# Sixty-two narrow products of zeros ahead of the first scores, three weight loads moved forward, and a new issue order in an attention and feed-forward kernel

## The chip, the core and the metric

The kernel runs on one core of a Trainium2 chip. The metric is the device time of one execution in microseconds; lower is better. TensorE (PE) multiplies, VectorE (DVE) and ScalarE (ACT) work elementwise and empty the accumulators, GpSimd (POOL) only builds an identity matrix, and SyncE (SP) issues every data transfer.

## What is computed

Chunked attention: every chunk of 32 queries looks at 8 memory keys and at the keys from 16 before the chunk to 8 behind it. Its output goes through a two-layer feed-forward block of width 2048 with a piecewise quadratic activation.

```
for c in range(nc):                                   # 24 chunks of 32 queries
    k_full = concat(mem_k, k[c*32-16 : c*32+32+8])    # v_full likewise
    a = softmax(q_c @ k_full.T / sqrt(64))
    out[c] = a @ v_full
x = out.transpose(0, 2, 1, 3).reshape(3072, 512)
h = x @ w_in                                          # 512 x 2048
g = where(h >= 1, h, where(h <= -1, 0, (h + 1)**2 / 4))
return g @ w_out                                      # 2048 x 512
```

## The kernel before, in words

The 3072 tokens are cut into six blocks of 512. Products are made as sums of three products of split operands (high and low parts), so each feed-forward slice of 128 hidden columns (called fc, 0 to 15) takes 12 products for the first layer and 12 for the second. Blocks 0 and 1 go this direct way. Blocks 2 to 5 use seven products in place of eight on combined operands (a fast 2 by 2 scheme), some of which are saved to and read back from device memory.

The order of all work is written out by hand in two tables of short names, and every engine keeps the order in which the program issues its instructions (class `InOrder`, line 132). `FIRST` (line 29) covers blocks 0 and 1 and the start of block 2, `PLAN` (line 63) the rest. Each name steps one small generator forward, and a step issues the instructions of one operation, mostly on one engine.

The names of `FIRST` that matter here:
- `+` issues the next transfer of the list `early` (line 1080): keys and queries of the first block in four groups, values, and the sixteen weight pieces of 1 MB (`load_w`), then the keys (`load_qk`, 1.5 MB) and values (`load_v`, 1 MB) of block 1.
- `g0` to `g3` are the four head groups of block 0 (`first_attention`): 64 score products; a reduction to the maximum; its subtraction; the exponential on ScalarE; sum, addition, reciprocal and multiplication on VectorE; 4 transposes on TensorE; a copy on ScalarE; 64 value products; and the high and low part of the result (`xth` on ScalarE, `xtl` on VectorE). g0 and g1 make the first half of the tokens of block 0, g2 and g3 the second.
- `w0` to `w15` decode a weight piece (`decode`): a scaling on ScalarE, three steps on VectorE, the high part on ScalarE, the low part on VectorE.
- `A0`, `A1`, ... and `B0`, ... are half steps of the feed-forward block for the first and the second half of block 0 (12 products of 256 columns, three activations, and later 6 products into the output); `E4`, ... are whole steps.

Ahead of both tables `keep_warm(8)` issues eight products of a tile of zeros (`warm`, bf16, 128x512) into one of the two `ps_h` accumulators, while the first keys are on their way.

In `PLAN`, `42p6` is product 6 of the third slice of block 4; `42c3` copies an accumulator into a tile `gt`, of which there are two (`copy_out`); `42a22` adds to it; `42r22` applies the activations; `42m22` joins them and sends the result to device memory (`keep`). The tile `gt` is taken by `c1`, `c3` and `r21`, and is free again after the matching `m`. Names with a `u` are the second layer of blocks 3 to 5 (`4u1q3` is one of its products), those with an `x` or a `y` the attention of a block.

Of the kernel before, what the change touches and what calls it, by code (L numbers as in the profile page):

```python
# [27 lines left out]

FIRST = """
    + + g0 g0 g0 + g0 g1 g0 + g0 g0 g1 g1 g0 g1 + g1 g0 w0 g1 g1 + g1 g0 w0 g1 w0 + g0 g1 w0 w0 g2  # L30
    + g0 w0 g1 w1 g2 g1 g2 g3 + g0 g2 g1 A0 g2 g3 g2 g3 + g3 A1 A0 g2 + g2 + g3 g2 g3 + A1 w1 w2 g3
    w1 g2 w3 A0 g3 + g3 w2 g3 w1 w2 g2 + g3 g2 g2 A0 g3 g3 A1 B0 + w2 w4 w1 w1 A0 B0 w3 + A2 B0 A1
    w2 B1 A1 A2 + w3 B0 w2 B1 B2 B1 w4 w3 B1 w5 A2 + B1 B0 w3 A0 A3 B0 w7 A2 A1 w4 w3 A2 B2 w5 B2
    w6 w4 + B2 w5 B2 B3 B1 A3 E4 w4 A3 + w8 w4 + B3 w5 E5 B2 w9 + A3 + E4 w6 B3 w5 A2 w6 E4 w6 B3
    A3 A3 w5 B3 w10 w6 w7 w11 E4 B3 w6 E5 w7 w8 + w7 E5 E7 w13 w7 E5 w12 E6 + w8 w14 E4 E6 w15 w7
    E4 w8 w9 E6 E5 E8 E5 w9 w8 w9 E6 E7 E6 w9 E7 w9 E8 E5 w8 E6 E9 E7 E7 w10 w11 w10 E7 E8 E4 E9
    w10 E8 w10 E6 E8 w11 w10 + w11 w12 w11 E9 E7 w12 E10 w11 E9 n0 E8 E9 E8 E10 w12 E10 E11 w13 w12
    E10 w12 w13 n0 E10 w13 E11 + E12 E11 w13 n0 E9 w14 n0 E10 E11 w13 E12 n0 n0 E9 E10 E11 E11 E11
    n0 n0 E12 n0 n0 n0 n0 + E13 n0 E12 n0 w14 E13 w15 E12 w14 n0 w15 n0 n0 E14 E12 n1 w14 n0 C0 w14
    w15 n1 E13 E15 n1 E14 E12 w15 E13 E14 E13 n1 n1 n1 E14 w15 n1 C0 E15 E14 n1 + n1 E15 n1 E13 n1  # L40
    n1 n1 C1 n1 C1 C0 E13 E15 C2 E14 E15 E14 C1 n1 E15 n1 C2 E15 C0 n1 n1 E15 E15 C0 D0 E15 C2 E15
    C1 D1 C3 D0 C0 C1 t0 C2 D1 D3 t0 D0 C1 D0 t0 C3 t0 D2 t0 t0 t0 D0 F5 D1 C2 t0 t1 D3 t1 t1 C3 t1
    C3 t1 C3 D1 D0 t1 D2 F4 D3 D1 D2 D3 C3 D1 t1 t2 F6 t1 t2 C2 D3 t2 D3 t2 D2 D2 F4 F4 F5 t2 t2 t3
    F5 t2 t2 t3 t3 F4 F5 t3 F6 D2 F4 t3 t3 F5 t4 F7 t4 n2 t3 F5 F4 t3 F4 F7 t4 F6 F6 F7 F6 t4 t4 t4
    t4 F5 t5 t5 t4 t5 t5 F7 t5 n2 t5 F7 F6 t6 t5 t6 t5 F8 F8 n2 n2 F8 n2 F7 t6 F9 t6 F9 n2 t6 t6 n2
    t6 F8 t7 n2 F8 F10 F9 F9 F6 t6 t7 F11 n2 n2 n2 F7 t7 n2 n2 + F9 t7 n2 t7 F10 F8 F11 t7 F8 t7
    F10 F12 F11 n2 F10 F10 F9 + n2 n3 t7 F12 n3 n3 F11 n3 n3 F13 n3 F10 F11 n3 F10 F12 F12 n3 F9
    F11 F12 n3 n3 F13 F13 F11 + n3 F12 n3 F13 n3 n3 n2 F14 F14 F14 n3 F13 F15 F12 n3 F14 F13 F14 n3
    n2 F13 F15 F15 F15 F15 n3
# [19 lines left out]
    22p6 T3 22a11 T3 3y 3y 22c2 22p7 22r11 3y 3y 22m11 22c3 3y 21m11 21g12 22h11 22p5 22a22 22p4
    22l11 22r21 22p3 3y 20g12 3y 23p1 T0 3y 3y T3 T3 T3 22m21 22a12 3y 22h21 23p2 22l21 3y T0 23c1  # L70
    23p6 21h11 21l11 23a11 22r12 22m12 T0 21g22 3y 3y 22r22 T0 T0 T0 T3 3kA11 T0 T0 22m22 3y 21g11
    T3 23p5 T0 T3 T3 3y 22h12 22l12 T4 T4 T4 T4 23c2 23p7 22h22 3kA12 22l22 23r11 3jA12 T3 22g11 T3
    T4 23c3 3y 23a22 3dS3 3kS3 23r22 23m11 23h11 T4 T2 23p4 3dS1 3dS2 23l11 T2 23r21 23p3 T2 T2 T2
    T2 22g21 23m22 T2 T2 3jA11 3kS2 23g11 23a12 T2 T2 3dS4 22g12 3kA22 3jS2 3jA22 23h22 3kS4 30p1
# [1136 lines left out]
```

## Time and profile before

| | us |
|---|---|
| median of three runs (585.54 to 586.42) | 586.1 |
| the profiled execution | 588.56 |
| its span, first to last instruction | 586.8 |
| TensorE busy | 568.6 (97%) |
| VectorE busy | 495.5 (84%) |
| ScalarE busy | 361.9 (62%) |

The share of busy time is a mean over very different stages. TensorE's idle time and its slower clock lie almost wholly in the first fortieths of the span; from 44 us on it is hardly ever idle. During the first four fortieths the DMA engines are busy without a break with the weights.

### The profile page before, as it was taken

Reading aid. Unit: us, or ns where it says so; the run is one execution under the profiler, and the core shown is the slowest. Engines: PE = TensorE matmul, PEld = TensorE weight load, DVE = VectorE, ACT = ScalarE, POOL = GpSimd, SP = SyncE. Lnnn points to the kernel's source line nnn. Section 1 sums busy time; section 2 is a strip of 40 time slices with the busy share of each in tenths; the row PEclk is TensorE's granted clock in tenths of the full one; section 3 lists DMA queues with packets and bytes.
Section 4 is the critical chain, followed back from the end, with each engine's and each line's share of the span. In section 5 each row is a group of like instructions: output and inputs, shape, how many; then the busy total and the mean of one; then the engine's idle time right before and its main releaser. Section 6 shows DMA issues by size and latency. Waiting matters only on the chain.

```text
span 586.8 us, 15427 instructions
## 1 busy us (share of the span) xinstructions
PE 568.6 (97%) x6504; PEld 516.6 (88%) x6504; DVE 495.5 (84%) x854; ACT 361.9 (62%) x667; POOL 0.7 (0%) x6
## 2 busy tenths in 40 slices
PE   5889999999999999999999999999999999999997
PEld 2788788889888889989888899999999999999997
DVE  5789999996989778687999689999887988666895
ACT  2489955446546446656685677576677565667652
POOL 0000000000000000000000000000000000000000
PEclk8579999999999999999999999999999999999999
DMA  8999103254976763474165798887898868887241
GB/s 351 421 422 418 77 0 109 71 165 145 341 279 237 271 240 120 164 275 163 55 251 170 259 311 307 299 300 268 286 287 283 290 205 301 286 255 249 90 151 48
DMA packets 39492, 135.21 MB, mean 230 GB/s; under 512 B 4096, under 2 KB 4096, under 8 KB 34816
## 3 DMA queue, kind: packets, MB, share of 16 engines
q1 hardware_dynamic: 39424, 134.23, 64.7%
q8 instruction: 51, 0.84, 0.6%
q14 instruction: 17, 0.14, 0.1%
HBM read 106.95 MB, written 27.26 MB: 229 GB/s over the span
## 4 chain that ended last, share of the span: by engine, by line
PE 83%; DVE 10%; DMA 3%; ACT 2%; issue 1%; DVEq 0%; SPq 0%; ACTq 0%
PE ps_o L140 38%; PE ps_h L140 37%; PE ps_x L140 4%; PE ps_s L140 3%; DVE gs L140 1%; DVE pr L140 1%; DMA gr<-plain_g 1%; PE ps_g L140 1%; DVE pt L140 1%; DMA wr<-saved 1%; DVE den L140 1%; DMA qk<-in_first_qk_dram 1%; DVE mx L140 1%; DVE ob L140 1%; DVE gk L140 1%
## 5 line engine op out<-in xcount | busy, mean ns | idle before, releaser
L140 PE MATMUL ps_o<-wr,gh 128*128 128x512 f32 x384 | 120.8, 396 | 0.0
L140 PE MATMUL ps_h<-s,wr 128*128 128x256 f32 x720 | 94.3, 283 | 0.7 <-ACT gt L140 0.4
L140 PE MATMUL ps_h<-xth,wr 128*128 128x512 f32 (+1 forms) x320 | 92.4, 364 | 0.0
L140 PEld LDWEIGHTS ps_h<-s,wr 128*128 128x128 f32 x720 | 89.4, 188 | 1.9 <-ACT gt L140 0.6
L140 PEld LDWEIGHTS ps_o<-wr,gh 128*128 128x128 f32 x384 | 70.5, 188 | 15.3 <-ACT ob L140 0.2
L140 PE MATMUL ps_o<-wr,gl 128*128 128x512 f32 x192 | 75.7, 394 | 0.0
L140 PE MATMUL ps_h<-a,wr 128*128 128x256 f32 x540 | 71.3, 283 | 0.5 <-DMA wr<-saved 0.5
L140 PEld LDWEIGHTS ps_h<-a,wr 128*128 128x128 f32 x540 | 67.6, 188 | 1.6 <-DMA wr<-saved 0.7
L140 PEld LDWEIGHTS ps_h<-xth,wr 128*128 128x128 f32 x320 | 59.5, 200 | 9.8 <-ACT gt L140 0.5
L140 PE MATMUL ps_h<-xtl,wr 128*128 128x512 f32 (+1 forms) x160 | 56.2, 362 | 0.1
L140 DVE SCALAR_TENSOR_TENSOR gw<-gw,gt 128x512 f32<-128x512 f32 (+1 forms) x76 | 47.6, 628 | 9.4 <-ACT gw L140 9.3
L140 ACT ACTIVATE gw<-ps_h 128x512 f32<-128x512 f32 (+1 forms) x55 | 29.6, 538 | 38.7 <-PE ps_h L140 26.2
L140 ACT ACTIVATE gw<-gw 128x512 f32<-128x512 f32 (+1 forms) x80 | 47.0, 588 | 0.0
L140 ACT CAST gh<-gw 128x512 fp32r<-128x512 f32 (+1 forms) x56 | 31.4, 563 | 22.0 <-DVE gw L140 22.0
L140 PEld LDWEIGHTS ps_o<-wr,gl 128*128 128x128 f32 x192 | 36.1, 188 | 8.5
L140 DVE STREAM_TRANSPOSE pt<-pr 32x512 f32<-32x512 f32 (+1 forms) x60 | 41.7, 701 | 1.3
L140 PE MATMUL ps_o<-wr,gsd 128*128 128x256 f32 x288 | 40.0, 282 | 0.0
L140 PE MATMUL ps_o<-wr,gsc 128*128 128x256 f32 x288 | 39.1, 281 | 0.0
L140 DVE SCALAR_TENSOR_TENSOR f<-w,f 128x1024 uint32<-128x1024 uint32 x32 | 38.8, 1219 | 0.1
L140 PE MATMUL ps_o<-wr,gsb 128*128 128x256 f32 x240 | 38.6, 282 | 0.0
L140 DVE TENSOR_TENSOR gl<-gw,gh 128x512 fp32r<-128x512 f32 (+1 forms) x56 | 34.0, 608 | 5.2 <-ACT gh L140 5.1
L140 PEld LDWEIGHTS ps_o<-wr,gsd 128*128 128x128 f32 x288 | 36.5, 188 | 0.2
(108 smaller groups left out, 959.6 us busy)
## 6 DMA issues: line engine op xcount, KB each, us to landing
wr<-saved SPq DMA_DIRECT2D x84, 512.0 KB, 4.9
w<-in_w_dram SPq DMA_DIRECT2D x16, 1024.0 KB, 19.8
qk<-in_qk_dram SPq DMA_DIRECT2D x10, 1536.0 KB, 8.0
v<-in_vw_dram SPq DMA_DIRECT2D x10, 1024.0 KB, 7.1
saved<-st SPq DMA_DIRECT2D x16, 512.0 KB, 3.6
wr<-saved SPq DMA_DIRECT2D x32, 256.0 KB, 4.1
saved<-wr SPq DMA_DIRECT2D x24, 256.0 KB, 4.7
plain_g<-gw SPq DMA_DIRECT2D x24, 256.0 KB, 5.2
```

The lines of the kernel that those rows point to most:

```text
L140: return self.tc.keep_in_program_order(getattr(self.engine, name)(*args, **kwargs))
```

## The change

- A new name `z` is the third entry of `FIRST`: it calls `fill(62)`, which issues 62 products of zeros, 32 columns of the stationary and 32 of the moving operand, into the other `ps_h` accumulator. They stand on TensorE behind the eight products of `keep_warm` and ahead of the first scores.
- Weight pieces 5, 6 and 7 are issued ahead of block 1's keys and values, not behind them.
- `FIRST` up to the end and all of `PLAN` stand in another order. `PLAN` holds the same 1160 names as before; `FIRST` has the same names and `z`. Of the 296 products that `PLAN` names, 51 keep their place in the row of products.

Cut to its core (of the tables, the first lines of `FIRST` and the lines of `PLAN` in which `42c3`, `42r22` and `42m22` stand):

```
+FILL = {"z": 62}
 FIRST = """
-    + + g0 g0 g0 + g0 g1 g0 + g0 g0 g1 g1 g0 g1 + g1 g0 w0 g1 g1 + g1 g0 w0 g1 w0 + g0 g1 w0 w0 g2
-    + g0 w0 g1 w1 g2 g1 g2 g3 + g0 g2 g1 A0 g2 g3 g2 g3 + g3 A1 A0 g2 + g2 + g3 g2 g3 + A1 w1 w2 g3
-    w1 g2 w3 A0 g3 + g3 w2 g3 w1 w2 g2 + g3 g2 g2 A0 g3 g3 A1 B0 + w2 w4 w1 w1 A0 B0 w3 + A2 B0 A1
-    w2 B1 A1 A2 + w3 B0 w2 B1 B2 B1 w4 w3 B1 w5 A2 + B1 B0 w3 A0 A3 B0 w7 A2 A1 w4 w3 A2 B2 w5 B2
+    + + z g0 g0 g1 g0 g0 + + g1 g0 g1 g0 g0 g1 g0 + g1 w0 w0 g0 + g1 g0 g0 w0 g1 w0 + + g0 g2 g1 g2
+    w0 g1 + g1 g1 g0 g2 g1 g2 w1 w0 g3 g1 A0 g2 A1 g3 g2 + + g3 + g3 g2 g2 g3 g2 g3 A0 g3 w1 g3 A0
+    w1 A1 g3 g2 g3 w2 A1 g2 g3 g2 w1 A1 + g2 g3 g3 w1 A0 + w2 + w3 w1 w4 w5 w2 w3 B0 B0 A0 + A2 w2
+    B0 + w2 w3 B0 A2 B0 w2 B1 w7 A0 B2 A1 B1 w3 w4 + w3 A3 B1 A2 w3 w4 + A2 B0 A1 B1 B1 A2 B2 w5 B2
...
 PLAN = """
...
-    3E6 4u0q7 3E7 4u0q5 4u0ld 4u0q6 3E5 4u0q3 4u1hb 4u1s3 4u1s1 4u1s2 42c3 42a22 42r11 42r22 4u1s4
-    42m11 42p4 4u0q4 4u1lb 4u1hd 42p3 4u1ld 4u1q2 42a12 4u1q6 4u1hc 4u1lc 42r21 43p1 4u1q3 42m22
...
+    4u1s2 4u1hc 4u1hb 4u1s4 4u1hd 4u1ld 42m11 5y 42p7 4u1lb 42c3 5y 4u1q2 5y 5y 4u1q3 42p4 42a22
+    42p3 4u1lc 4u1q5 5y 5y 4u1q7 5y 42r21 43p1 42a12 5y 4u0q4 42r12 42m21 42m12 4u2s3 4u2s1 43c1
...
+    5kS1 5jS1 4u3q6 4u0la 50c1 4u3q3 50a11 4u0q1 5kA22 5jA22 4u3hc 50p6 4u3lc 4u5s3 4u3q5 4u3q4
+    4u5ha 4u3q7 5kS3 4u5s1 5jS3 4u4r 4u3la 42r22 50c2 4u5s2 4u3q1 50p7 5dS4 4u5s4 5kS4 42m22 50p5
...
+    def fill(n):
+
+        ps = ps_h.tile([P, 512], F32, name="ps_h")
+        for _ in range(n):
+            pe.matmul(ps[0:32, 0:32], warm[:, 0:32], warm[:, 0:32], start=True, stop=True)
...
-        (load_w, 2), (load_w, 3), (load_w, 4), (load_qk, 1, 0), (load_v, 1, 0),
+        (load_w, 2), (load_w, 3), (load_w, 4), (load_w, 5), (load_w, 6), (load_w, 7), (load_qk, 1, 0), (load_v, 1, 0),
     ]
-    early += [(load_w, i) for i in range(5, NPW)]
+    early += [(load_w, i) for i in range(8, NPW)]
...
+        if name in FILL:
+            fill(FILL[name])
+            continue
```

## Rows read from the trace of the kernel before

**Rows 1.** The page's first and third part: busy time of the engine, its share of the span and its instructions (PE multiplies, PEld loads stationary operands); the DMA queue that carries instructions for the busiest engine: packets, MB, share.

```profile
PE 568.6 (97%) x6504; PEld 516.6 (88%) x6504; DVE 495.5 (84%) x854; ACT 361.9 (62%) x667; POOL 0.7 (0%) x6
q8 instruction: 51, 0.84, 0.6%
```

**Rows 2.** Stretches of the span: length, busy time and instructions of each engine, granted TensorE clock as a share of full, DMA share and GB/s. Up to where TensorE stops, up to the first output product, the long middle, and the end.

```profile
0.00:21.12 21.12, 12.91 (x349) 8.79 (x349) 12.80 (x23) 8.45 (x11) 0.70 (x6) 0.71 0.92 372
0.00:43.40 43.40, 31.54 (x608) 26.28 (x609) 30.53 (x51) 21.77 (x39) 0.70 (x6) 0.69 0.97 398
44.00:582.00 538.00, 535.78 (x5891) 489.33 (x5890) 463.25 (x800) 339.88 (x628) 0.00 (x0) 1.00 0.63 218
582.00:586.80 4.80, 0.68 (x6) 0.47 (x4) 1.18 (x3) 0.00 (x0) 0.00 (x0) 0.89 0.29 109
```

**Rows 3.** TensorE's waits from 44 us on: what, for whom, us in total, times, the longest.

```profile
PE ps_o L140 <- DVE gsa L140: 0.5, 1, 0.5
PE ps_h L140 <- DMA wr<-saved: 0.5, 1, 0.5
PE ps_h L140 <- ACT gt L140: 0.4, 1, 0.4
```

**Rows 4.** Timeline of the front, TensorE's products (start, length, count; in brackets the idle time before them): the zeros, then scores (ps_s), transposes (ps_h from ident) and values (ps_x) of the groups g0 to g3, and the first product of A0.

```profile
1.19 3.60 PE L140 MATMUL ps_h<-warm 128*128 128x512 bf16 x8 [1.19 <-DVE warm L140]
5.15 0.99 PE L140 MATMUL ps_s<-qk 64*32 64x64 f32 x64 [0.36 <-DMA qk<-in_first_qk_dram]
7.04 0.86 PE L140 MATMUL ps_s<-qk 64*32 64x64 f32 x64 [0.90 <-DMA qk<-in_first_qk_dram]
11.91 1.09 PE L140 MATMUL ps_h<-ident,pr 128*128 128x128 f32 x4 [4.02 <-DVE pr L140]
14.88 1.94 PE L140 MATMUL ps_x<-pt,v 64*64 64x32 f32 x64
16.75 1.18 PE L140 MATMUL ps_s<-qk 64*32 64x64 f32 x64
17.86 1.93 PE L140 MATMUL ps_x<-pt,v 64*64 64x32 f32 x64
23.06 1.06 PE L140 MATMUL ps_s<-qk 64*32 64x64 f32 x51 [1.94 <-issue]
24.05 0.58 PE L140 MATMUL ps_h<-xth,wr 128*128 128x256 f32 x1
```

**Rows 5.** The transfers in the stretch from 20.4 to 21.6 us, by queue: packets, MB, share of 16 engines.

```profile
q1 hardware_dynamic: 63, 0.48, 98.8%
q8 instruction: 1, 0.02, 5.3%
```

**Rows 6.** What was asked of the tile `warm`: its loads as stationary operand (ns shortest, median, longest).

```profile
L140 PEld LDWEIGHTS <-warm x8: 106/152/152, 1.2 to 3.7; 128*128 128x128 bf16 x8
```

**Rows 7.** Timeline of VectorE in the front: the sum of g0, the reduction of g1, the multiplication of g0, one step of decoding w0, the last two parts of g0 and g1.

```profile
8.48 0.69 DVE L140 TENSOR_REDUCE den<-pr 128x8 f32<-128x512 f32 x1 [0.69 <-ACT pr L140]
9.75 0.69 DVE L140 TENSOR_REDUCE mx<-ps_s 128x8 f32<-128x512 f32 x1
11.09 0.68 DVE L140 TENSOR_TENSOR pr<-pr,rin 128x512 f32<-128x512 f32 x1
14.36 2.48 DVE L140 SCALAR_TENSOR_TENSOR f<-w,f 128x1024 uint32<-128x1024 uint32 x2
20.48 1.28 DVE L140 TENSOR_TENSOR xtl<-ps_x,xth 128x512 fp32r<-128x512 f32 x2
36.25 0.69 DVE L140 TENSOR_TENSOR xtl<-ps_x,xth 128x512 fp32r<-128x512 f32 x1 [1.11 <-ACT xth L140]
```

**Rows 8.** Timeline from 29 us on, TensorE: transposes of g2 and g3, values of g2 and g3, the first product of B0.

```profile
29.34 0.63 PE L140 MATMUL ps_h<-ident,pr 128*128 128x128 f32 x4
30.29 0.66 PE L140 MATMUL ps_h<-ident,pr 128*128 128x128 f32 x4 [0.31 <-ACT gt L140]
32.06 1.35 PE L140 MATMUL ps_x<-pt,v 64*64 64x32 f32 x64 [1.12 <-ACT pt L140]
33.63 1.94 PE L140 MATMUL ps_x<-pt,v 64*64 64x32 f32 x64 [0.21 <-ACT pt L140]
35.49 0.58 PE L140 MATMUL ps_h<-xth,wr 128*128 128x256 f32 x1
```

**Rows 9.** The same stretch on ScalarE: the last activation of A1, then scaling w2, the copy of g2, scaling w3, the copy of g3.

```profile
30.12 0.42 ACT L140 ACTIVATE gw<-gw 128x256 f32<-128x256 f32 x1
30.43 1.11 ACT L140 ACTIVATE w<-w 128x1024 f32<-128x1024 f32 x1
31.43 0.58 ACT L140 COPY pt<-ps_h 128x512 f32<-128x512 f32 x1
31.89 1.22 ACT L140 ACTIVATE w<-w 128x1024 f32<-128x1024 f32 x1
32.97 0.61 ACT L140 COPY pt<-ps_h 128x512 f32<-128x512 f32 x1
```

**Rows 10.** Stretches cut where the granted clock changes (columns as in group 2).

```profile
8.93:29.40 20.47, 13.80 (x289) 12.39 (x290) 16.98 (x32) 8.24 (x13) 0.00 (x0) 0.50 1.02 421
29.41:32.81 3.40, 1.97 (x61) 1.49 (x59) 1.84 (x3) 3.24 (x6) 0.00 (x0) 1.00 1.00 420
32.82:39.64 6.82, 6.54 (x109) 6.04 (x102) 5.71 (x8) 4.87 (x10) 0.00 (x0) 0.50 1.02 426
39.65:585.70 546.05, 540.80 (x5929) 494.07 (x5927) 468.77 (x810) 343.58 (x638) 0.00 (x0) 1.00 0.63 219
```

**Rows 11.** The waits of SyncE's queue for transfers of weights (us in total, times, the longest), and the time from issue to landing of the weight pieces (us shortest, median, longest).

```profile
SPq L140 <- DMA w<-in_w_dram: 19.3, 9, 2.3
DMA to landing us min/median/max: 8.6/19.8/21.3
```

**Rows 12.** What was asked of the tile `gt` (ns shortest, median, longest): the copy, the addition, the activation and the joining step.

```profile
L140 ACT COPY gt<-ps_h x30: 566/586/592, 226.4 to 541.9; 128x512 f32<-128x512 f32 x30
L140 DVE TENSOR_TENSOR gt<-gt,ps_h x30: 678/681/689, 227.9 to 546.4; 128x512 f32<-128x512 f32 x30
L140 ACT ACTIVATE gt<-gt x32: 632/633/638, 230.9 to 547.8; 128x512 f32<-128x512 f32 x32
L140 DVE SCALAR_TENSOR_TENSOR gw<-gw,gt x76: 415/684/693, 29.0 to 559.0; 128x512 f32<-128x512 f32 x60, 128x256 f32<-128x256 f32 x16
```

More of the change, by code (lines that the diff above doesn't have):

```diff
@@ L40 @@
[L40 to L49, printed above, removed]
+    A3 A3 w5 B3 w10 w6 w7 w6 w7 B3 w11 E4 + w8 w7 E5 E7 w13 E5 E4 w7 E5 w12 E6 + w8 w14 E6 w15 w7
@@ L50 @@
+    F10 F12 t7 t7 F11 n2 F10 F10 F11 F9 n3 n2 t7 n3 + n3 F12 n3 n3 F13 F10 F11 F12 F12 n3 n3 n3 F10
+    F9 F11 F12 n3 n3 F11 F13 n3 F13 n3 F13 + n3 F12 n3 F14 F13 F14 F14 n3 n2 n3 F15 F12 F14 F13 F14
+    n3 n2 F13 F15 F15 F15 F15 n3
 """
@@ L69 @@
[L69 to L74, printed above, removed]
@@ new lines @@
+    3kA11 T3 T3 T3 T3 22m12 23a11 23p5 21g22 22h21 22l21 22g21 3y 3y 3y 3kA12 3y 3y 3y 3y 23r11
+    23m11 23h11 3y 23c2 3y 3y 23p7 23l11 22h12 3y T3 T3 T4 22g11 22l12 T4 23c3 23p4 23a22 23p3
+    23g11 T3 22g12 T3 23r22 3dS3 3jA12 23m22 4x T3 T3 3dS1 T3 3dS2 3jA11 T3 T4 T4 T4 23r21 23m21
+    23h22 23l22 23a12 30p2 3dS4 3kS2 23g22 T4 30p1 T2 3kS1 21g12 3jS2 23h21 23l21 3kS4 T2 T2 T2 T2
+    T2 23r12 23m12 22r22 22m22 T2 T2 3kS3 3jS3 3kA22 3jS1 T4 T4 4x 22h22 T2 T2 T2 T4 30c1 30a11
+    22l22 23h12 23l12 T4 3jA22 T4 3jS4 T5 T5 T5 30p6 T2 30c2 30p5 30p7 30r11 30m11 30c3 30a22 30r22
@@ new lines @@
+    4x T5 T5 23g12 4x T5 30p3 30a12 T5 2z0 30p4 30m22 T5 23g21 30r21 4x 4x 4x T5 T5 30m21 32p1 T5
+    22g22 2z1 31p1 4x 30r12 31p2 31c1 4x 4x 30m12 3u0hb 31p6 31c2 31a11 4x 4x 4x 31p5 31r11 4x
+    3u0s3 3u0s1 31p7 3u0s2 3u0hc 31c3 3u0s4 31m11 T5 31a22 32p2 31p4 3u0hd 3u0ld 31r22 3u0lb 31m22
+    31p3 32c1 32a11 31a12 4x 32p6 3u0lc 31r21 3u0q5 3u0q6 T6 T6 T6 3u0q3 31r12 31m12 3u0q7 3u1s3
+    3u1s1 3u1s2 3u0q2 32r11 3u1s4 31m21 32c2 32p7 32p5 32m11 T6 4x T6 T6 3u1hd 3u1ld 3u1hc 3u1lc
+    3u1q6 3u0q4 3u1q3 T6 32c3 32a22 32p3 T7 T7 T7 32r22 T7 32p4 T6 4y T7 3u1hb T7 3u1lb T6 T6 T7
@@ new lines @@
+    3u6r 3D0 3D1 3D2 3D4 3u4ha 3D3 3u4la 3D6 40p1 3u4q1 3u4hd 3u4hb 3u4lb 3u4q4 4kA22 3u4ld 3D7
+    3u4q2 3D5 3D8 3u4q3 3u4q6 4jA22 3u5r 3u4hc 4kS1 5x 33m22 3u4lc 4kS3 3u4q7 40c1 4dS2 4kS2 3u4q5
+    40a11 4jS2 3u6s3 3u6s1 3u6s2 3u6hc 4jS1 40p6 3u6lc 3u6q5 4jS3 3u6q7 5x 40c2 40p7 3u6hb 3u6s4
+    3u5s3 3u5s1 3u5hc 3u5s2 40p5 3u6lb 3u6q4 3u5lc 3u5q5 5x 40r11 33m21 4dS4 3u6q2 3u5s4 40m11
+    3u5hb 40c3 3u5q7 40p4 3u5lb 3u5q2 3u5q4 4kS4 4jS4 5x 40a22 40p3 3u6ha 3u6la 3u6q1 40r21 40m21
+    3u5hd 3u5ld 3u5q6 5x 3u7r 3u5q3 3u5ha 40a12 3u5la 41p1 5x 5x 5x 40r12 41c1 41p2 40m12 41a11
@@ L129 @@
+    5u5q1 5u5lb 5u5q4 5u5hd 5u5ld 5u5q2 5u5q6 5u5q3 5u5hc 5u5lc 5u6r 5u5q7 5u6s3 5u6ha 5u6la 5u6s1
+    5u5q5 5u6hb 5u6s2 5u6s4 5u6lb 5u6q4 5u6hd 5u6hc 5u6ld 5u6q3 5u7r 5u6lc 5u7s3 5u6q6 5u6q7 5u7s1
+    5u7s2 5u7s4 5u7ha 5u7la 5u6q5 5u6q2 5u7hb 5u7lb 5u7q1 5u6q1 5u7hd 5u7ld 5u7q2 5u7q4 5u7hc 5u7q6
+    5u7lc 5u7q5 5D8 5E0 5E1 5E2 5E4 5u7q7 5E3 5E6 5E7 5u7q3 5E5 5E8
 """
```

112 lines of the change are left out of this document (50 added, 62 removed).

## The prediction

> **What bounds the kernel.** I read three views, in this order. First the stretches: from 44 to 582 us TensorE is busy 535.78 of 538.00 us, so only 2.22 us of idle time are left there, while in the first 43.40 us it is busy 31.54, idle 11.86, and at a mean granted clock of 0.69 [rows 2]. The end holds 4.80 us, mostly the last additions and the last store. Second the waits behind 44 us: the three longest take 0.5, 0.5 and 0.4 us [rows 3]; no single one is worth a change. Third the timeline of the front, since only there is time to be had. The amount of TensorE's work is the same on both sides (the zeros apart), so the end moves by what the front gains, plus or minus a change in the 2.22 us.
>
> In the front the reader sees four losses. TensorE waits 4.02 us for g0's probabilities [rows 4]. It stops for 1.94 us in the middle of g3's scores, after 13 of 64, and no engine releases it ("issue") [rows 4]; at that point it had run 349 products and 349 loads [rows 2]. Between 29.34 and 35.49 it waits for two copies that ScalarE makes behind two scalings of weights [rows 8, 9]. And the clock is granted at 0.50 (1.2 of 2.4 GHz) from 8.93 to 29.40 and from 32.82 to 39.64, for good at 1.00 only from 39.65 on [rows 10].
>
> The 1.94 us are a wait for code, as I read them. TensorE has 6504 products and 6504 loads, and queue 8 brings 51 instruction packets [rows 1], that is 255 instructions for each, or some 127 products with their loads. One of these packets is on the way between 20.4 and 21.6 us, beside a data queue that fills 98.8% of the 16 engines [rows 5]. If the stop at 349 is the end of a packet, the end before it is at 349 - 128 = 221, the 13th or 14th of g2's scores (they are 208 to 271), at 16.75 + 14 x 0.018 = 17.0 us. From there to the restart at 23.06 are 6.05 us: my estimate of how long a packet takes here from being asked for, when the one before it is used up, until it can run.
>
> The Trainium skill says in "Runtime: NRT & Kernel Launch", section "Instruction fetch mechanics", that engines refill their code in blocks of 256 instructions and that crossing a block's border is mostly hidden. The count of the trace agrees with the 256, the stop of 1.94 us does not agree with "hidden". By that rule no border would cost anything in the new order either: this is rival 2 below, 582.4 us.
>
> **The change, part by part.**
>
> *The 62 products of zeros.* They start when the eight wide ones end, at 1.19 + 3.60 = 4.79 us. The trace has no product of this shape. Below: like g1's scores, 0.86 / 64 = 13.4 ns each, 0.83 us. Above: every product waits for a load as long as those of the zeros, 0.152 us each [rows 6], 9.4 us. I take 30 ns, the rate of the value products, 1.93 / 64 [rows 4], because they too have 32 columns: 1.9 us, end at 6.7. g0's scores, at 5.15 today, then start 1.5 us later. Beside them goes the shift: 62 products with 62 loads are 124 instructions, about half a packet.
>
> *The order of g0 and g1.* Today VectorE idles 0.69 us before g0's sum and takes g1's reduction, 0.69, ahead of g0's multiplication [rows 7]. In the new order g1's reduction fills the idle time: multiplication at 11.09 + 1.52 - 0.69 = 11.9. The transposes follow 0.82 later at 12.7; today g1's transposes stand between g0's and its values, in the new order they don't, so the values come after 1.09 (transposes) and 0.59 (copy) and some 0.1 of handing over: 14.5, against 14.88. g1 comes later: behind g0's multiplication VectorE now has g1's sum, addition and reciprocal and the three steps of w0 ahead of g1's multiplication, with that some 4.7 us by steps of 0.69 and 1.24 [rows 7]; it ends at 12.6 + 4.7 = 17.3, transposes and copy to 19.2, values from 19.3, against 17.86.
>
> *Where the packets end.* In the new stream the borders are at the same counts: 221 falls on the 19th of g0's values (202 to 265), at 14.5 + 19 x 0.030 = 15.1; the next packet is there at 15.1 + 6.05 = 21.2. The border at 349 falls on the 15th of g1's values (334 to 397), which would be reached at 19.75. So the stop is not gone: 1.45 us by this sum. Both its ends carry about 1 us of doubt (the zeros, the 6.05), so the bounds are 0 and some 2.5. I take half of the sum, 0.7. With the whole 1.45, g1's values end at 22.7, and 0.6 for each of the two parts [rows 7] lets A0 start at 24.0, as today (24.05); with none it starts at 22.6. Value taken: 23.3, a gain of 0.7. The border at 477 is in A1, 3 products in; its packet is there by about 27.2, when A1 gets there: nothing.
>
> *The copies of g2 and g3.* Here the gain is plain. Today ScalarE does, after A1's activations, 1.11 for w2, copy of g2 at 31.43, 1.22 for w3, copy of g3 from 32.97 to 33.58 [rows 9]. In the new order both copies come first: g2's at 30.43, g3's at 31.0, when its transposes end (30.29 + 0.66). g2's values start at 31.1, g3's at 31.1 + 1.35 = 32.4 against 33.63 [rows 8], B0 at about 34.2 against 35.49, and g3's low part ends at 35.6 against 36.94 [rows 7]: 1.3 us earlier, on top of A0's gain.
>
> *The clock.* It comes back after 4.15 us of unbroken wide products today (35.49 to 39.64). If it follows the work, the whole gain stays; if it comes back at the same moment, what runs earlier runs at half speed, and half of the gain is lost. I take the first, since before 29.40 too it rose behind a run of wide products; the second is rival 3.
>
> *The weight pieces.* Today pieces 5 to 7 wait behind 2.5 MB. At 421 GB/s [rows 10] these are 5.9 us; the new order needs it because ScalarE scales w5 ahead of B0's activations. The keys and values that go back by 3 MB, 7.1 us, are first used by block 1's scores at 88 us: no cost, covered by some 50 us. On SyncE's queue the values of block 1 waited for g1's values to be read; with three pieces ahead of them that wait now holds up nothing earlier. The queue waits for weight transfers nine times anyway, and a piece takes 19.8 us from issue to landing [rows 11]: the engines stay full, the total is the same.
>
> *The second table.* The products are the same. Today's idle time is 2.22 us; the new order can bring it to 0 or add waits of the size of those that are there, 0.2 to 0.5 us each. I leave it at 2.2, with bounds 0 and 4.4. VectorE, busy 463.25 of 538 us [rows 2], and the transfers at 0.63 cover the moves that I followed: the stores and reads of block 4's third slice lie some 8 us of products ahead of their use.
>
> *Sum.* Against the profiled execution: span 586.8 - 0.7 - 1.3 = 584.8, and 588.56 - 2.0 = 586.6 for its time. That execution was 2.46 above the median; against the median 586.1 - 2.0 = 584.1. Own range of this case 583.2 to 585.0.
>
> **Rivals.**
> 1. *Slower: the later table makes TensorE wait.* In the new order 42r22 stands 119 names behind 42c3, with five other uses of `gt` (42r21, 43c1, 43c3, 43r21, 50c1) in between; today it is 3 names. One of the two `gt` tiles is held all that time, so those five go through a single tile, each for copy, addition, two or three activations and the joining step: 0.59 + 0.68 + 3 x 0.63 + 0.68 = 3.8 us [rows 12]. It decides from the point at which the next copy has to wait longer than the products that stand between them (a slice has seven, about 1.4 us each, so there is room of 6 us); at about 0.8 us for each of five the loss is 4, less the front's 2.0: 588.1. For it: VectorE and ScalarE lag when outside work comes between. Against it: 43r22 and 33r22 are held back today, and the waits are 0.5 at most [rows 3]. Chance 0.15.
> 2. *No border costs anything in the new order.* As a mechanism here: the packet is asked for earlier than I count, or g1's values are later than 21. Then A0 gains 1.45, the copies 1.3, and about 1 us more comes from a clock that rises sooner: 586.1 - 3.7 = 582.4. For it: only one such stop is in the whole trace of before. Against it: g0's values come earlier than g2's scores, so the packet has no longer time than today. Chance 0.20. It is the outcome that the section of the Trainium skill named above would lead one to expect.
> 3. *The shift does not do what it is for.* The stop moves from g3's scores to g1's values at its full 1.45 us, A0 starts as today, and the clock comes back at the same moment, so that of 1.3 us half is left: 586.1 - 0.65 = 585.4. For it: the sum above gives exactly that. Chance 0.27.
>
> **How the numbers follow.** Forecast 0.38 (584.1). A time further than 0.2% (1.2 us) from the median is about what a measurement of this kernel can tell from no change. Faster: nine tenths of the forecast and rival 2, 0.54. Same: rival 3 and the rest of the forecast, 0.30. Slower: rival 1, and 0.01 for zeros that cost their upper bound. The range leaves out the far part of rival 2 and most of rival 1: 581.8 to 587.3.
>
> **What would show it.** The zeros: their length behind 4.79, and g0's scores near 6.7. The packets: an idle stretch marked "issue" inside g1's values, none in g3's scores. The copies: g3's values and B0 1.2 us or more earlier than A1's end explains. The clock: the last change to 1.00, before or at 39.6. The second table: idle time of TensorE from 44 us on near 2.2. I am wrong if that idle time moves by more than the front does, or if the zeros push g0 so far back that A0 comes later than 24.05.

## The result and the profile after

| | before | after |
|---|---|---|
| median of five runs, us | 585.54 (585.12 to 586.42) | 589.21 (588.82 to 589.89) |
| ratio, 95% interval | | 1.0055 (1.0039 to 1.0071) |
| the profiled execution, us | 588.56 | 588.89 |

The changed kernel is slower by 0.55%. Forecast were 584.1 us and a range up to 587.3; the time lies outside, on the other side. The two profiled executions differ by 0.33 us only, though the medians differ by 3.67: the execution of before on which the prediction rests stands 3.0 us above the median of these runs, the one of after 0.3 below its own. So the two traces can't be set against each other as they are, and the first experiment is a second trace of the kernel before. A "packet" here and below is one of the instruction packets of queue 8, a "border" the count of products at which one packet ends and the next begins, and a "stop for code" idle time of TensorE that no engine and no transfer releases ("issue").

The page of after, first and third part, and TensorE's waits over the whole span (what, for whom, us in total, times, the longest):

```profile
PE 568.0 (97%) x6566; PEld 515.9 (88%) x6566; DVE 493.4 (84%) x854; ACT 361.5 (62%) x667; POOL 0.7 (0%) x6
q8 instruction: 52, 0.85, 0.6%
```
```profile
PE ps_x L141 <- issue: 4.2, 2, 3.8
PE ps_h L141 <- DVE pr L141: 4.2, 1, 4.2
PE ps_x L141 <- ACT pt L141: 1.4, 2, 0.7
```

62 products more, one packet more, and two stops without a releaser, together 4.2 us, both in value products (`ps_x`). The timeline of TensorE's products in the front of after (start, length, count; in brackets the idle time before them) has them at 19.68 and 34.02:

```profile
1.19 5.26 PE L141 MATMUL ps_h<-warm 128*128 128x512 bf16 x70 [1.19 <-DVE warm L141]
6.38 1.53 PE L141 MATMUL ps_s<-qk 64*32 64x64 f32 x128
...
13.86 1.93 PE L141 MATMUL ps_x<-pt,v 64*64 64x32 f32 x64 [0.68 <-ACT pt L141]
...
18.62 0.65 PE L141 MATMUL ps_x<-pt,v 64*64 64x32 f32 x16 [0.68 <-ACT pt L141]
19.68 1.51 PE L141 MATMUL ps_x<-pt,v 64*64 64x32 f32 x48 [0.41 <-issue]
...
22.23 0.58 PE L141 MATMUL ps_h<-xth,wr 128*128 128x256 f32 x1
...
25.59 0.28 PE L141 MATMUL ps_h<-xtl,wr 128*128 128x256 f32 x1
...
26.67 0.60 PE L141 MATMUL ps_h<-ident,pr 128*128 128x128 f32 x4
27.66 0.63 PE L141 MATMUL ps_h<-ident,pr 128*128 128x128 f32 x4 [0.39 <-ACT gt L141]
28.36 1.82 PE L141 MATMUL ps_x<-pt,v 64*64 64x32 f32 x109
34.02 0.85 PE L141 MATMUL ps_x<-pt,v 64*64 64x32 f32 x19 [3.84 <-issue]
34.80 0.58 PE L141 MATMUL ps_h<-xth,wr 128*128 128x256 f32 x1
...
52.44 0.40 PE L141 MATMUL ps_h<-xth,wr 128*128 128x512 f32 x1
```

To be read against [rows 4, 8]: up to A0, at 22.23 against 24.05, the front is ahead. Then 109 of g3's and g2's 128 value products run in 1.82 us, and TensorE stands for 3.84 us ahead of the last 19. This is product 603 counted from the start; the stops in [rows 4] and at 19.68 are at 349 and 350. From 350 to 603 are 253 products, two packets of about 127; the border between them, 477, is passed in A1, with the product at 25.59. The packet behind 603 is on the way when TensorE has stood for over a microsecond. The transfers of after from 31.4 to 32.6 us, by queue (packets, MB, share of 16 engines), beside full data queues as in [rows 5]:

```profile
q1 hardware_dynamic: 72, 0.48, 99.4%
q8 instruction: 1, 0.02, 5.3%
```

Stretches of after, columns as in [rows 2]: the front, TensorE's standing, two cut where the granted clock changes, the long middle, the end:

```profile
0.00:43.40 43.40, 31.43 (x664) 26.04 (x665) 29.20 (x50) 22.03 (x38) 0.70 (x6) 0.76 0.97 398
30.19:34.02 3.83, 0.00 (x0) 0.00 (x0) 0.96 (x2) 0.61 (x2) 0.00 (x0) 0.78 1.02 419
25.49:32.30 6.81, 4.23 (x128) 3.67 (x128) 5.59 (x10) 4.58 (x11) 0.00 (x0) 1.00 1.01 421
32.31:39.13 6.82, 5.07 (x37) 4.71 (x37) 3.60 (x5) 4.22 (x6) 0.00 (x0) 0.50 1.01 423
44.00:582.00 538.00, 535.46 (x5897) 489.04 (x5896) 462.13 (x802) 338.85 (x630) 0.00 (x0) 1.00 0.64 218
```

The clock, granted at 1.00 from 25.49, falls to 0.50 at 32.31, while TensorE stands, and is at 1.00 again from 39.14. Up to 43.40 TensorE has done 664 products, against 608 in [rows 2], of which 62 are zeros: six products less of real work. From 44 us on it is idle for 538.00 - 535.46 = 2.54 us, against 2.22.

VectorE's multiplication of g0 and low part of g3, and ScalarE's two copies (start, length, count):

```profile
11.26 0.69 DVE L141 TENSOR_TENSOR pr<-pr,rin 128x512 f32<-128x512 f32 x1
35.53 0.69 DVE L141 TENSOR_TENSOR xtl<-ps_x,xth 128x512 fp32r<-128x512 f32 x1 [4.31 <-ACT xth L141]
```
```profile
27.72 1.19 ACT L141 COPY pt<-ps_h 128x512 f32<-128x512 f32 x2
```

The copies of g2 and g3 are made at once as their transposes end, where [rows 9] had scalings between. Both value groups could run through from 28.36; the packet doesn't let them.

### The profile page after: what moved, and what is told of

Read it like the earlier page. It is cut to its first block, busy times and chain, and to the rows that moved or that the text cites. A ratio compares the mean times of both kernels' runs of the same rounds, so it can differ in the third digit from the quotient of the medians.

```text
span 587.1 us, 15532 instructions
## 1 busy us (share of the span) xinstructions
PE 568.0 (97%) x6566; PEld 515.9 (88%) x6566; DVE 493.4 (84%) x854; ACT 361.5 (62%) x667; POOL 0.7 (0%) x6
## 4 chain that ended last, share of the span: by engine, by line
PE 83%; DVE 10%; ACT 3%; issue 2%; DMA 1%; DVEq 0%; ACTq 0%
PE ps_o L141 39%; PE ps_h L141 36%; PE ps_x L141 5%; DVE f L141 3%; PE ps_s L141 2%; DVE wr L141 1%; DVE pr L141 1%; PE ps_g L141 1%; DMA wr<-saved 1%; DVE gw L141 1%; ACT gw L141 1%; DVE mx L141 1%; DVE feo L141 0%; DVE ob L141 0%; DVE pt L141 0%
## 5 line engine op out<-in xcount | busy, mean ns | idle before, releaser
L141 ACT ACTIVATE gw<-ps_h 128x512 f32<-128x512 f32 (+1 forms) x55 | 29.5, 536 | 32.6 <-PE ps_h L141 24.3
```

The costliest lines, as they stand in the source:

```text
L141: return self.tc.keep_in_program_order(getattr(self.engine, name)(*args, **kwargs))
```

## Experiments

**Theory 1**: the loss lies in the front. The code packet behind product 603 comes too late for g3's value products, and the clock falls in that stop; the prediction's base was moreover an execution later than usual. **Theory 2**, the rival: the front is no worse than before usually, and the loss lies in the rest of the new order, above all in its second table. Where an experiment asks something narrower, its expectation says what each theory means there. "E4" is the start of E4's first product, the first whole step, at which all of the front is done; "idle" is 534.00 less TensorE's busy time between 44 and 578 us. The medians of before that the ratios are taken against are 585.68 to 585.93 (for after 585.54).

| kernel | median, us | ratio (95%) | stops for code up to 44 us | E4 | idle |
|---|---|---|---|---|---|
| before, again | 585.74 | 1.0000 (0.9988 to 1.0013) | 0.93 | 48.73 | 1.78 |
| after | 589.21 | 1.0055 (1.0039 to 1.0071) | 0.41, 3.84 | 52.44 | 2.54 |
| new FIRST, old PLAN | 592.01 | 1.0105 (1.0087 to 1.0123) | 0.57, 0.62, 3.48 | 52.74 | 3.22 |
| old FIRST, new PLAN | 589.49 | 1.0054 (1.0037 to 1.0072) | 1.5 | 49.60 | 3.44 |
| after without zeros | 588.30 | 1.0051 (1.0034 to 1.0067) | 0.61 | 47.54 | 4.48 |
| the same with old PLAN | 584.79 | 0.9979 (0.9969 to 0.9989) | 1.3 | 48.95 | 2.67 |
| that, w4 and w5 later | 584.77 | 0.9983 (0.9971 to 0.9996) | 0.9 | 47.91 | 3.65 |
| before with zeros | 593.94 | 1.0134 (1.0108 to 1.0160) | 2.06, 0.27, 2.98 | 54.28 | 4.53 |
| after, zeros at 110 us | 585.45 | 0.9993 (0.9983 to 1.0003) | 0.8 | 47.70 | 2.38 |
| old loads | 590.01 | 1.0069 (1.0052 to 1.0087) | 0.98 | 53.34 | 2.59 |
| after, 30 zeros | 584.41 | 0.9982 (0.9968 to 0.9997) | 0.87 | 47.61 | 3.58 |
| loads only | 586.06 | 1.0001 (0.9987 to 1.0014) | 1.51 | 50.25 | 2.06 |

Stops, starts and idle times are of one execution each, which can stand up to 1.6 us off the median beside it.

### Before, again

The kernel before, with an empty line more at its end:

```diff
+
```

> The kernel before, unchanged, to see how its front goes in other executions than the one that was read: the execution read (588.56 us) lies 3.0 us above the median of the timed ones (585.54). Theory 1, what a code packet costs differs from execution to execution in the kernel before: the front of this profile is 1 to 3 us shorter, with the stop in g3's scores well under 1.94 us or the clock at 1.00 earlier than 39.6 us. Theory 2, the front is always the same and the 3 us lie behind 44 us or outside the span: the stop is 1.9 again, the clock comes back at 39 to 40 us, and idle time from 44 us on differs.

Median 585.74. Of its trace, the longest stop for code, the stretch in which the read execution of before had a clock of 0.50 [rows 10], and the first products of A0, B0 and E4:

```profile
PE ps_s L140 <- issue: 0.9, 1, 0.9
```
```profile
25.80:39.60 13.80, 11.23 (x194) 9.81 (x193) 13.01 (x21) 12.60 (x27) 0.00 (x0) 1.00 1.01 424
```
```profile
22.89 0.58 PE L140 MATMUL ps_h<-xth,wr 128*128 128x256 f32 x1
...
32.41 0.39 PE L140 MATMUL ps_h<-xth,wr 128*128 128x256 f32 x1
...
48.73 0.40 PE L140 MATMUL ps_h<-xth,wr 128*128 128x512 f32 x1
```

The same kernel, and the stop in g3's scores is 0.93 us, not 1.94; the clock comes back at 25.7 for good, and E4 starts 3.11 us earlier than in the read execution (51.84). Against this trace after loses: at A0 it is 0.66 ahead (22.23 against 22.89), at B0 2.39 behind (34.80 against 32.41), at E4 3.71 behind. So the 3.84 us of standing, less what the copies gave, cost 3.05, and between B0 and E4, with the clock at half up to 39.13, another 1.32 are lost. The spans differ by 587.1 - 582.4 = 4.7: 3.7 of it is the front.

The repeated execution is itself a quick one, 584.14 us where its median is 585.74, so 3.7 is at the upper end. Two other traces have the front of before: old FIRST with new PLAN, traced at its median, has E4 at 49.60, and loads only, which moves three loads besides, at 50.25. Against these, after is 2.8 and 2.2 behind. In all three the clock is at 1.00 from 25.7 to 28.2 us on and stays there through the front; only the read execution falls back to 0.50 in it. So the stop differs from execution to execution, as Theory 1 of this run has it, and after loses in its front against each of the three. Whether the new order without that stop would be good is open.

### New FIRST with old PLAN, and old FIRST with new PLAN

The changed kernel (zeros and moved loads too) with the `PLAN` of before; cut to the first line of each table:

```diff
-FIRST = """
-    + + g0 g0 g0 + g0 g1 g0 + g0 g0 g1 g1 g0 g1 + g1 g0 w0 g1 g1 + g1 g0 w0 g1 w0 + g0 g1 w0 w0 g2
+FIRST = """
+    + + z g0 g0 g1 g0 g0 + + g1 g0 g1 g0 g0 g1 g0 + g1 w0 w0 g0 + g1 g0 g0 w0 g1 w0 + + g0 g2 g1 g2
...
 PLAN = """
     20p1 20p2 20c1 20a11 2dS4 2kS4 2jS4 20p6 20c2 3x 20p7 3x 3x 20r11 20m11 20p5 20c3 20p4 L0 3x
...
```

> The changed front (zeros, loads, first table) with the old second table. Theory 1, the loss is the 3.84 us stop for a code packet in g3's values in the front: as slow as the changed kernel, 588.5 to 589.5 us. Theory 2, the new second table makes TensorE wait: as fast as before or faster, 584 to 586 us.

592.01 us. TensorE's waits, the longest for code in the front's values and in the second table's output products:

```profile
PE ps_x L141 <- issue: 4.2, 3, 3.5
...
PE ps_o L141 <- issue: 1.1, 1, 1.1
```

The front is as in after (stop of 3.48 at product 603, E4 52.74). The old second table now has stops for code of its own, 0.17, 1.07 and 0.41 (at 359.9, 395.4 and 444.4 us), where before had none.

The kernel before, with its loads and without zeros, with the new `PLAN`:

```diff
 FIRST = """
     + + g0 g0 g0 + g0 g1 g0 + g0 g0 g1 g1 g0 g1 + g1 g0 w0 g1 g1 + g1 g0 w0 g1 w0 + g0 g1 w0 w0 g2
...
-PLAN = """
-    20p1 20p2 20c1 20a11 2dS4 2kS4 2jS4 20p6 20c2 3x 20p7 3x 3x 20r11 20m11 20p5 20c3 20p4 L0 3x
+PLAN = """
+    20p2 2dS4 20p1 20c1 20a11 L0 20p6 20c2 2kS4 2jS4 3x 3x 3x 20p7 20c3 20p5 3x 20p4 20a22 20r22
...
```

> The old front with the new second table. Theory 1 (the loss is in the front): 585 to 586 us, within 0.2% of before. Theory 2 (the loss is in the second table): 588 to 589.5 us.

589.49 us. Its two longest waits for code:

```profile
PE ps_s L140 <- issue: 1.5, 1, 1.5
...
PE ps_x L140 <- issue: 1.3, 1, 1.3
```

The first is the old one, of the front. The second is at 350.51 us, in value products of the second table, and the clock is granted at 0.50 behind it from 350.8 to 354.2. Each half of the change alone is as slow as the whole, or slower. Neither theory says that; what the halves share is that the second table stands at another distance from the start of TensorE's instructions than in the kernel it comes from: the old one is moved by 62 products, the new one lacks them. That this is the cause is a guess so far; the next runs test it.

### The zeros taken out, with the new and the old PLAN

```diff
-FILL = {"z": 62}
+FILL = {"z": 0}
```

> The changed kernel with no zeros, all else alike. Theory 1, packets end at fixed counts of the stream (about 221, 350, 476 and 603 products), so that without the zeros each border falls 62 products later in the program: the 3.84 us stop in g3's values is gone (the border at 603 lies among wide products), a stop of 1 to 2 us stands after 13 or 14 of g3's scores as in the kernel before, and the time is 586 to 588 us. Theory 2, the stop in g3's values belongs to the new order and not to the count: it stays at about 3.8 us after 109 of 128 value products, and the time stays at 588.5 to 589.5.

588.30 us, above what Theory 1 gave, although the front does what it said: no stop in g3's values, and E4 at 47.54, 4.90 earlier than in after (the stop in g3's scores, given as 1 to 2 us, is 0.61). What is won there is lost from 44 us on. TensorE's waits in that stretch, and the stretch behind the first of them:

```profile
PE ps_x L141 <- issue: 1.3, 1, 1.3
...
PE ps_o L141 <- issue: 0.7, 1, 0.7
PE ps_h L141 <- issue: 0.7, 1, 0.7
```
```profile
348.90:352.30 3.40, 3.40 (x17) 3.40 (x17) 3.33 (x8) 1.62 (x4) 0.00 (x0) 0.50 0.91 311
```

Three stops for code, 2.6 us together, and 3.40 us at half the clock. None of them is in after.

The new `FIRST` and loads without zeros, with the `PLAN` of before:

```diff
+FILL = {"z": 0}
 FIRST = """
-    + + g0 g0 g0 + g0 g1 g0 + g0 g0 g1 g1 g0 g1 + g1 g0 w0 g1 g1 + g1 g0 w0 g1 w0 + g0 g1 w0 w0 g2
+    + + z g0 g0 g1 g0 g0 + + g1 g0 g1 g0 g0 g1 g0 + g1 w0 w0 g0 + g1 g0 g0 w0 g1 w0 + + g0 g2 g1 g2
...
```

> The new first table and the loads, without the zeros, with the old second table, so that every code packet of the second table ends where it did in the kernel before. Theory 1 (what costs time is where packets end among narrow products): no stops for code from 44 us on, idle time there near 2 us, and the front 1.2 us shorter than before's in its usual course (product 656 counted without the zeros at 47.5 against 48.7 us): 584.0 to 584.9 us. Theory 2 (the new first table leaves VectorE and ScalarE behind, and the later stages pay): idle time from 44 us on rises to 4 us and more, 586 to 588 us.

584.79 us, ratio 0.9979 (0.9969 to 0.9989): faster than before and after. Old PLAN without zeros has no stops for code from 44 us on here, as in before. The front that was to be 1.2 us shorter is not in this trace: E4 is at 48.95, in an execution 1.3 us above its median. The traced execution of new PLAN without zeros, 588.30, is 2.2 us longer than this one, 586.11: from 44 us on it has 1.81 us more idle time and loses some 1.7 in the 3.40 us at half the clock, in which TensorE was busy throughout, and its E4 is 1.41 earlier. The four cases are: zeros and new PLAN 589.21, zeros and old PLAN 592.01, no zeros and new PLAN 588.30, no zeros and old PLAN 584.79. With the old table the zeros cost 7.2, with the new one 0.9. So neither the zeros nor the new table has a cost of its own that could be added to the other's.

### The scalings of w4 and w5 later

In both kernels without zeros TensorE waits 1.7 us for B0's activations, which stand behind three scalings of weights on ScalarE.

```diff
-    w1 A1 g3 g2 g3 w2 A1 g2 g3 g2 w1 A1 + g2 g3 g3 w1 A0 + w2 + w3 w1 w4 w5 w2 w3 B0 B0 A0 + A2 w2
+    w1 A1 g3 g2 g3 w2 A1 g2 g3 g2 w1 A1 + g2 g3 g3 w1 A0 + w2 + w3 w1 w2 w3 B0 B0 w4 w5 A0 + A2 w2
```

> As no_fill_old_plan, with ScalarE's scalings of w4 and w5 put behind B0's activations. In the run without zeros TensorE waits 1.69 us for B0's activations, which stand behind the scalings of w3, w4 and w5 (31.77 to 35.02 us). Theory 1, that wait is lost time: 0.8 to 1.7 us faster than no_fill_old_plan, 583 to 584 us. Theory 2, VectorE's decoding bounds the front and the wait only comes later: within 0.5 us of it.

584.77 us against 584.79: nothing. The wait for B0's activations is gone, and 1.52 us at 38.64, ahead of B2, and 0.43 behind it stand in its place. ScalarE has the same work to do; the scalings put later make TensorE wait later. E4 is 1.04 us earlier than in the run above (47.91), but idle time behind it is 0.98 longer, of which 0.66 are two stops for code in scores, 0.24 at 197.65 and 0.42 at 367.03. The same table at the same distance has none in before, before again, loads only, old loads and without zeros with old PLAN. So a stop's place is not fixed by the distance alone.

### The zeros alone

`fill` as in the change, called from a place of its own:

```diff
     keep_warm(8)
+    fill(62)
```

> The kernel before with the 62 zeros ahead of the first scores and nothing else. Theory 1 (packets): the borders fall 62 products earlier in the program: about 15 into g1's values, in A1, and about 45 into g3's values, where a stop of 2 to 4 us stands; in the second table stops of some 1.7 us in all, as with the changed front and the old second table; 588.5 to 592 us. Theory 2, the zeros cost only their own 1.6 us, which the wait for the first keys and for g0's probabilities covers in part: 585.7 to 587.3 us.

593.94 us, more than either theory gave. Its longest waits for code:

```profile
PE ps_x L140 <- issue: 5.0, 2, 3.0
...
PE ps_o L140 <- issue: 1.4, 1, 1.4
```

In the old order too the zeros bring stops into the narrow value products (2.06 at 349 in g1's, 2.98 at 603 in g3's) and stops further on (0.90 at 122.6 us, 1.35 at 211.0), which before hasn't. The zeros are enough to make the front's loss; the new order isn't needed for it.

### A quiet data queue at the time of the packet

The changed kernel, with weight piece 5, and what stands behind it on SyncE's queue, held back until VectorE has written g3's low part: in `load_w`, VectorE first writes a column of the piece's tile, in its own order. Late weights are the price, so that only the length of the stop at 603 is read.

```diff
+            if i == 5:
+                dve.memset(raw[i][:, 0:1], 0)
```

> The changed kernel, with weight piece 5 and all transfers behind it held back until VectorE has made g3's low part (a one-column write into the piece's tile ahead of its load), so that the data queue runs dry at about 25 us, when the packet behind product 603 is asked for. Theory 1, the packet waits behind queued data: the stop at 603 shrinks from 3.84 us to under 1.5. Theory 2, the time of a packet does not depend on the data queue: the stop stays at 3.5 us or more. The whole kernel is slower, since the weights come late; its time decides nothing.

One execution, 592.73 us. The stretch from 28 to 30 us in this kernel, and then in after (last columns: clock, DMA share, GB/s), and this kernel's stops for code in value products:

```profile
28.00:30.00 2.00, 1.57 (x61) 1.23 (x60) 2.00 (x5) 2.00 (x6) 0.00 (x0) 1.00 0.14 49
```
```profile
28.00:30.00 2.00, 1.93 (x112) 1.69 (x111) 2.00 (x3) 1.98 (x4) 0.00 (x0) 1.00 1.01 422
```
```profile
PE ps_x L141 <- issue: 1.7, 2, 1.3
```

The stop at 603 is 1.29 us in place of 3.84. From the product behind the border at 477 to going on behind 603 it takes 32.30 - 26.43 = 5.9 us, in after 34.02 - 25.59 = 8.4. The trace has the packet's own transfer too. Counted from the border at 477, here it starts after 3.09 us (at 29.52), takes 1.38 with no data beside it, and 1.40 later TensorE goes on; in after it starts after 5.90 (at 31.49), takes 1.02, and TensorE goes on after 1.51. So the shorter stop comes from 2.81 us less of waiting ahead of the transfer, and 1.29 us stay though the queue is nearly empty: the products between the two borders last 4.4 us, the packet 5.9.

Full queues alone don't make 5.9 us of waiting, though. In after the packet asked for at the border at 350 (and needed at 477) waits 3.46 us until its transfer starts, the one asked for at 477 (and needed at 603) 5.90, and both stretches are full of data (columns as in [rows 2]):

```profile
19.68:23.14 3.46, 3.46 (x116) 3.22 (x117) 1.54 (x4) 1.88 (x3) 0.00 (x0) 0.50 1.06 438
25.59:31.49 5.90, 4.13 (x127) 3.58 (x127) 5.49 (x10) 4.48 (x10) 0.00 (x0) 1.00 1.01 421
```

What makes the second wait longer no run shows; data ahead of the packet have a part in it, since without them it is 3.09.

### The zeros at 110 us

The same zeros from a tile of their own, ahead of E14: both new tables, the second table shifted as in after, the front not.

```diff
-    + + z g0 g0 g1 g0 g0 + + g1 g0 g1 g0 g0 g1 g0 + g1 w0 w0 g0 + g1 g0 g0 w0 g1 w0 + + g0 g2 g1 g2
+    + + g0 g0 g1 g0 g0 + + g1 g0 g1 g0 g0 g1 g0 + g1 w0 w0 g0 + g1 g0 g0 w0 g1 w0 + + g0 g2 g1 g2 w0
...
-    n0 n0 E12 n0 n0 n0 E13 + E12 n0 n0 n0 w14 E12 n0 E13 w15 w14 w15 n0 E14 n0 E12 w14 n0 w14 w15
+    n0 E13 + E12 n0 n0 n0 w14 E12 n0 E13 w15 w14 w15 n0 z E14 n0 E12 w14 n0 w14 w15 n1 n1 E15 C0 E14
...
-            pe.matmul(ps[0:32, 0:32], warm[:, 0:32], warm[:, 0:32], start=True, stop=True)
+            pe.matmul(ps[0:32, 0:32], zeros, zeros, start=True, stop=True)
```

> The changed kernel, loads and both tables, with the same 62 products of zeros (from a small tile of their own) put ahead of E14's first layer at about 110 us, not ahead of the first scores. Theory 1 (packets): the front goes as without zeros (E4's first product at about 47.5 to 49 us, no stop in g3's values), and the second table, whose packets then end as in the changed kernel, has no stop for code; the zeros cost about 1.6 us of TensorE, which is busy there: 585 to 586.5 us, against 589.2 of the changed kernel. Theory 2, the new second table loses by itself, wherever packets end: 588 us or more.

585.45 us, ratio 0.9993 (0.9983 to 1.0003). E4 starts early, and there is no stop for code from 44 us on (idle 2.38 against 4.48 without zeros):

```profile
47.70 0.40 PE L141 MATMUL ps_h<-xth,wr 128*128 128x512 f32 x1
```

This tells the two effects of the zeros apart. In the second table the shift takes the stops for code away: 588.30 becomes 585.45. At the front the same products cost 589.21 - 585.45 = 3.76 us more than at 110 us.

### Thirty zeros

```diff
-FILL = {"z": 62}
+FILL = {"z": 30}
```

> The changed kernel with 30 products of zeros, not 62. Theory 1 (packets end at fixed counts): with 32 products fewer, the border at 350 falls 48 into g1's values, that at 476 falls 14 into g2's values, and that at 603 among wide products, so that no 3.8 us stop stands in g3's values; in the second table, laid out for 62, stops of 0.5 to 3 us in all come back: 586.5 to 589 us. Theory 2, the zeros themselves (their time ahead of the first scores) are what costs in the front: the front's loss is half of that of 62, in proportion.

584.41 us, ratio 0.9982 (0.9968 to 0.9997), below what was expected. Product 603 is now among B0's wide products, behind all the narrow ones, and the stop there is short:

```profile
PE ps_h L141 <- issue: 0.9, 1, 0.9
```

E4 starts at 47.61. The second table's stops, expected to come back with half the shift, did not: there is none from 44 us on (its idle time of 3.58 us is waits for transfers and for other engines, 1.5 of it for saved products read back). So not one distance only is good for the new table.

### The loads

The kernel without zeros and with old PLAN, pieces 5 to 7 again behind block 1's keys and values, all of these issued behind w2's first step, so that none is missing when w5 needs it:

```diff
-    w1 A1 g3 g2 g3 w2 A1 g2 g3 g2 w1 A1 + g2 g3 g3 w1 A0 + w2 + w3 w1 w4 w5 w2 w3 B0 B0 A0 + A2 w2
-    B0 + w2 w3 B0 A2 B0 w2 B1 w7 A0 B2 A1 B1 w3 w4 + w3 A3 B1 A2 w3 w4 + A2 B0 A1 B1 B1 A2 B2 w5 B2
+    w1 A1 g3 g2 g3 w2 A1 g2 g3 g2 w1 A1 + g2 g3 g3 w1 A0 + w2 + + + + w3 w1 w4 w5 w2 w3 B0 B0 A0 A2 w2
+    B0 w2 w3 B0 A2 B0 w2 B1 w7 A0 B2 A1 B1 w3 w4 w3 A3 B1 A2 w3 w4 + A2 B0 A1 B1 B1 A2 B2 w5 B2
...
-        (load_w, 2), (load_w, 3), (load_w, 4), (load_w, 5), (load_w, 6), (load_w, 7), (load_qk, 1, 0), (load_v, 1, 0),
+        (load_w, 2), (load_w, 3), (load_w, 4), (load_qk, 1, 0), (load_v, 1, 0),
```

> As no_fill_old_plan (new first table, no zeros, old second table, 584.8 us), with weight pieces 5 to 7 behind block 1's keys and values again; the first table issues these loads four names earlier in a row so that each piece is still issued ahead of its use. Theory 1, the earlier loads are needed by the new order, since ScalarE scales w5 ahead of B0's activations: piece 5 lands 6 us later, B0's activations wait, 0.5 to 3 us slower. Theory 2, the loads are no part of the effect, the pieces land in time anyway: within 0.5 us.

590.01 us against 584.79. ScalarE's waits between 28 and 50 us, and TensorE's longest over the span:

```profile
ACT w L141 <- DMA w<-in_w_dram: 5.5, 2, 4.6
```
```profile
PE ps_h L141 <- ACT gt L141: 7.9, 3, 6.3
```

ScalarE waits for the piece ahead of B0's activations, TensorE behind it, and the clock is granted at 0.50 from 37.6 to 44.4. The new order can't do without the moved loads; the cost, 5.2 us, was larger than expected.

The kernel before with the moved loads alone (the same lines as in the change):

> The kernel before with weight pieces 5 to 7 ahead of block 1's keys and values, nothing else. Theory 1, the order of the loads alone moves nothing, since the old order does not ask for the pieces earlier and the keys are used at 88 us: within 0.2% of before. Theory 2, more weights queued behind each other make code packets wait longer: the stop in g3's scores grows and the time rises by 1 us or more.

586.06 us, 1.0001 (0.9987 to 1.0014): they cost nothing and bring nothing by themselves.

## Why the prediction was wrong

**The step that failed** stands in "Where the packets end": "The border at 477 is in A1, 3 products in; its packet is there by about 27.2, when A1 gets there: nothing", and the count of borders ended there. The place was right (three products into A1, at 25.59). But the packet that counts is the one asked for at that border, needed at the next, 603, 109 products into the values of g3 and g2. In between lie only nine products of A1, eight transposes and those 109, which the gain worked out for the copies lets run without a break. The sum has no term for this packet: it stands at nothing without a reason. What the runs show in its place is the stop of 3.84 us.

Its size could not have been read off the prediction's own times. By these the packet, asked for at 27.2, is there at 27.2 + 6.05 = 33.3, and its place is reached 45 products into g3's values, at 32.4 + 45 x 0.030 = 33.8: no stop, by half a microsecond. Both of these times were off. The border was passed at 25.59 and the values began at 28.36, not 31.1, with A0 earlier by 1.07 us and the clock at 1.00 from 25.49 on (in [rows 10] from 29.41). With 6.05 us from 25.59 the packet is there at 31.6, and the products reach its place at 30.2: a stop of 1.5 us. The other 2.4 are the packet's 8.4 us in place of 6.05.

**The clock.** "If it follows the work, the whole gain stays" was the right idea: it did follow, and so it fell in the new stop (0.50 from 32.31 to 39.13), and by E4 1.32 us more were lost. In the forecast it only ever rose sooner.

**The base.** The sum was made against an execution 3.0 us above the median. I subtracted gains from that execution and carried the difference over to the median. In the three other traces of that front the clock doesn't fall back once it has risen behind A0, and the stop at 349 is 0.93 to 1.51, so part of what the new order was to gain isn't lost there to begin with: the repeated trace has B0 at 32.41, ahead of the 34.2 that I forecast for the changed kernel.

**Right in mechanism and about in size.** The zeros: 5.26 - 3.60 = 1.66 us for 62, 27 ns each against 30, end at 6.45 against 6.7. g0's multiplication 11.26 (11.9), its values 13.86 (14.5), g1's 18.62 (19.3). The stop in g1's values, 0.41 where 0.7 was taken and 1.45 was the sum. A0 at 22.23, earlier than the 23.3. That it is 0.66 earlier than in the repeated trace, where a gain of 0.7 was forecast, is chance: A0 is 1.07 off, and that base is 1.16 off the one that the forecast used. The copies: nothing but the packet stood between transposes and B0; without zeros and with old PLAN, B0's first product is at 31.29. The loads: no cost by themselves; needed by w5.

**The second table.** Left at 2.2, it came out at 2.54, so the term was right for after. The reason given was incomplete: I looked at waits on tiles and transfers, but the runs show that either second table has stops for code at some shifts and few or none at others, 0.17 to 1.35 us each. Part of the rest of the 4.7 us is the end: from the last product to the end of the span it is 4.6 us in after, 4.1 in the repeated trace, with one addition of VectorE more behind it, by the two rows. That wasn't in the sum:

```profile
581.91 1.65 DVE L141 TENSOR_TENSOR ob<-ob,ps_o 128x256 f32<-128x256 f32 x4
```
```profile
577.62 1.21 DVE L140 TENSOR_TENSOR ob<-ob,ps_o 128x256 f32<-128x256 f32 x3 [0.36 <-PE ps_o L140]
```

(VectorE's last instructions, in after and in the repeated trace of before.)

**The rivals.** Rival 1 had the direction and nearly the time, 588.1, by a mechanism that didn't happen: TensorE's waits for ScalarE's `gt` from 44 us on are few and short, in after 0.7 at most:

```profile
PE ps_g L141 <- ACT gt L141: 0.7, 1, 0.7
```

Rival 2, no border costs anything, is refuted by the stop that ends at 34.02. What the Trainium skill says in "Runtime: NRT & Kernel Launch", section "Instruction fetch mechanics", that a border is mostly hidden, agrees with most borders here: of 52 packets in after two show a stop. It doesn't agree with the two in the front, 0.41 and 3.84 us. Rival 3, the stop only moves, came nearest in kind, but in it the stop kept its size and went to g1's values.

**Left open.** Why the packet behind 603 waited 5.90 us ahead of its transfer and the one before it 3.46, both among data: the quiet queue shows that data have a part in it, not which. Which distances are good for a second table: 0 for the old and 30 or 62 for the new one are nearly free of stops, by runs; a rule was not tried for.
